# Attention with mixed heads and a gated MLP on one core: the second mixing runs two steps behind the first

## The chip, the cores and the metric

The kernel runs on one core of a Trainium2 chip. The metric is the device time of one execution in microseconds; where several runs are shown, their median. The profile names the engines PE (TensorE, with PEld for its weight loads), DVE (VectorE), ACT (ScalarE), POOL (GpSimd) and SP (SyncE, which issues most DMAs here).

## The reference

Attention over four batches, twelve heads, 448 positions and head size 64, in which the heads are mixed twice: the scores by `w_pre` ahead of the softmax, the weights by `w_post` behind it. Its output is the input of a normalised, gated MLP.

```
scores = scale * matmul(q, k.T)                       # per head
scores = einsum('bhij,hg->bgij', scores, w_pre)       # first mixing
attn   = exp(scores - max) / (sum + 1e-9)             # softmax over j
attn   = einsum('bhij,hg->bgij', attn, w_post)        # second mixing
x      = matmul(attn, v)      -> (1792 tokens, 768)
xn     = x / sqrt(mean(x*x) + 1e-6) * rms_g
out    = (silu(xn @ w_gate) * (xn @ w_val)) @ w_out   # 768 -> 1536 -> 768
```

## The kernel before

**Chunks and steps.** The query rows of a batch are cut into four chunks (120, 120, 120 and 88 rows), sixteen chunks in all (`n` = 0 to 15). A chunk is worked off in steps `p` (six, and five in the last chunk of a batch), 92 steps in all. `steps` numbers them, and `first[n]` is the number of the first step of chunk `n`: `first[14]` is 81 and `first[15]` is 87. `part_a` runs a loop over `t`, and one turn of it is called step t here.

**A turn of the loop.** The order in which the turns issue their instructions is each engine's order; nothing moves them afterwards. In turn t stand, on their engines:

- `premix` (line 187): TensorE's first mixing of step t, into two banks `sp`. Woven into it are the score matmuls `qk_mm` (line 140) of a later chunk, whose two banks `qk` go out through `qk_evac`: one half as `st` on ACT (line 162), the other on DVE (line 160). SP then lays the `st` tiles into the rows `r` of a later step by DMA (line 179).
- `rowmax` (DVE, line 196: two negated row maxima `nm`), `expo` (ACT, line 203: two tiles `e` of exponentials, and their sums), and `norm`: on DVE `t` and `rp` (lines 210, 212), on POOL two tiles `wn` (line 215), which are `w_post` scaled by the reciprocal of the sums.
- `postmix` (line 226): the second mixing, of step t-1, 56 matmuls with `e` as the loaded weights and `wn` as the moving operand, into two banks `pm`. `evac_a` copies one of them to `at_all` on ACT (line 265), the other on DVE (line 263).
- `av_mm` (line 294): the product with v, in units that `av_at` lays out over the turns. A block is two chunks (the last two chunks are blocks of their own) and has twelve units, two for each pair of heads. After four units the two banks `av` are full, and ACT copies them to `xt` (lines 304, 306, 308); the copy stands at the head of the turn after the units.
- POOL adds and squares `xt` (lines 318 to 333) for the sums that the normalisation needs, and SP stores `xt` (lines 340, 343). `sq_all` turns the column sums of a batch (`pss`, line 347, on TensorE) into reciprocal roots, in small operations over several turns.

PSUM has two banks for each of `qk`, `sp`, `pm` and `av`, so that each of these waits for the copies or exponentials of what it held before. In SBUF four tiles `e` are kept.

**After the loop's end** comes part B, the MLP (lines 741 to 752 on TensorE). Its first weights and factors are prepared by DVE, ACT and POOL in the last turns of the loop.

## Time and profile before

| what | value |
| --- | --- |
| median of 3 runs | 827.72 us (825.3 to 830.05) |
| the profiled execution | 822.48 us |
| its span in the trace | 820.6 us |
| PE busy | 794.4 us, 97% of the span |
| DVE busy | 634.5 us, 77% |
| ACT busy | 507.3 us, 62% |
| POOL busy | 350.4 us, 43% |
| mean granted clock of TensorE | 0.998 |

The span is from the first to the last instruction in the trace; that execution took 1.9 us more than its span. The loop over the steps runs from 20.1 us to about 339 us of the span, and the MLP from there to the end. A busy share is an average over both.

### The profile page before, as it was taken

The page shows a single profiled execution, that of the slowest core. Times are in us where ns is not written, and L with a number is a line of the kernel's source. Part 1 is how long each engine was busy: PE and PEld are TensorE (multiplying, and loading weights), DVE is VectorE, ACT ScalarE, POOL GpSimd, SP SyncE. Part 2 cuts the span into 40 slices and gives each one's busy share as a digit, 9 for nine tenths or more (in the row PEclk, how much of TensorE's full clock was granted, in tenths as well). Part 3 has the DMA queues.
Part 4 walks back from the last instruction along what each step waited for, and adds up shares of the span by engine and source line. Part 5 has one row for each costly group of instructions (what it writes and reads, how often), then busy time and mean ns, then how long its engine had stood idle before and what let it go on. Part 6 is the DMA issues. An engine that isn't in the chain of part 4 may idle for free.

```text
span 820.6 us, 26914 instructions
## 1 busy us (share of the span) xinstructions
PE 794.4 (97%) x10806; PEld 485.2 (59%) x10806; DVE 634.5 (77%) x1322; ACT 507.3 (62%) x1133; POOL 350.4 (43%) x467
## 2 busy tenths in 40 slices
PE   7899999999999989899999999999999999999998
PEld 2567777767776767655555555555555555555555
DVE  5777878888798867888788978997889676547562
ACT  3677778777776867664344454545444546969850
POOL 7212343454355435843624433426144359452310
PEclk9999999999999999999999999999999999999999
DMA  7777777777876754564255644754546446566641
GB/s 216 208 216 217 219 229 222 228 219 232 222 234 200 211 147 150 158 230 118 66 177 150 183 129 127 216 149 121 174 145 201 133 127 184 157 199 176 184 135 67
DMA packets 81902, 145.15 MB, mean 177 GB/s; under 512 B 10527, under 2 KB 72797, under 8 KB 81779
## 3 DMA queue, kind: packets, MB, share of 16 engines
q1 hardware_dynamic: 79982, 139.83, 57.0%
q0 software_dynamic: 832, 2.06, 1.0%
q8 instruction: 85, 1.39, 0.7%
q10 hardware_dynamic: 965, 1.56, 0.6%
q14 instruction: 38, 0.31, 0.1%
HBM read 72.83 MB, written 31.88 MB: 128 GB/s over the span
## 4 chain that ended last, share of the span: by engine, by line
PE 86%; DMA 8%; DVE 2%; issue 1%; ACT 1%; POOL 1%; SPq 0%; ACTq 0%; DVEq 0%; POOLq 0%
PE qk L140 7%; PE pm L226 7%; PE sp L187 7%; PE av L294 6%; PE pg L750 6%; PE pg L752 6%; PE pv L752 6%; PE pg L751 6%; PE pv L751 6%; PE pv L750 6%; DMA r<-st 6%; PE po L751 6%; PE po L750 6%; PE po L752 6%; DMA wraw<-in_wgv 1%
## 5 line engine op out<-in xcount | busy, mean ns | idle before, releaser
L187 PE MATMUL sp<-r,wk_pre 64*64 64x448 f32 x720 | 167.4, 542 | 5.4 <-DMA r<-st 3.5
L203 ACT ACTIVATE e<-sp,nm 128x448 f32<-128x448 f32 x180 | 114.3, 637 | 84.8 <-DVE nm L196 82.4
L140 PE MATMUL qk<-k,q 64*64 64x448 f32 x768 | 152.6, 559 | 5.9 <-DMA q<-in_q 4.1
L196 DVE TENSOR_REDUCE nm<-sp 128x1 f32<-128x448 f32 x180 | 110.3, 620 | 44.1 <-PE sp L187 27.4
L215 POOL TENSOR_SCALAR wn<-wk,rp 128x60 f32<-128x60 f32 x180 | 59.5, 345 | 181.8 <-DVE rp L212 109.7
L226 PEld LDWEIGHTS pm<-wn,e 60*64 60x64 f32 x5040 | 106.1, 134 | 37.6 <-POOL wn L215 23.8
L226 PE MATMUL pm<-wn,e 60*64 60x60 f32 x5040 | 106.7, 220 | 4.2 <-issue 4.1
L798 POOL TENSOR_TENSOR sg<-sg,u 128x448 f32<-128x448 f32 x36 | 45.9, 1275 | 151.2 <-ACT sg L795 106.7
L294 PE MATMUL av<-at_all,v 64*64 64x240 f32 (+6 forms) x1728 | 93.6, 316 | 4.6 <-issue 2.6
L750 PE MATMUL pv<-x,wh 128*128 128x448 f16 x264 | 93.0, 352 | 0.0
L752 PE MATMUL pv<-x,wl 128*128 128x448 f16 x264 | 93.0, 352 | 0.0
L752 PE MATMUL pg<-x,wl 128*128 128x448 f16 x264 | 93.0, 352 | 0.0
L751 PE MATMUL pv<-x,wh 128*128 128x448 f16 x264 | 93.0, 352 | 0.0
L751 PE MATMUL pg<-x,wh 128*128 128x448 f16 x264 | 93.0, 352 | 0.0
L750 PE MATMUL pg<-x,wh 128*128 128x448 f16 x264 | 93.0, 352 | 0.0
L750 PE MATMUL po<-h,fac 128*128 128x448 f16 (+1 forms) x258 | 89.8, 348 | 0.0
L751 PE MATMUL po<-h,fac 128*128 128x448 f16 (+1 forms) x258 | 89.8, 348 | 0.0
L752 PE MATMUL po<-h,fac 128*128 128x448 f16 (+1 forms) x258 | 89.8, 348 | 0.0
L750 PEld LDWEIGHTS <-wh 128*128 128x128 f16 x528 | 51.7, 98 | 48.2 <-issue 0.2
L751 PEld LDWEIGHTS <-wh 128*128 128x128 f16 x528 | 51.7, 98 | 48.3 <-issue 0.3
L752 PEld LDWEIGHTS <-wl 128*128 128x128 f16 x528 | 51.7, 98 | 48.2
L187 PEld LDWEIGHTS sp<-r,wk_pre 64*64 64x64 f32 x720 | 60.3, 133 | 27.2 <-ACT e L203 13.2
(167 smaller groups left out, 1567.3 us busy)
## 6 DMA issues: line engine op xcount, KB each, us to landing
r<-st SPq DMA_DIRECT2D x117, 210.0 KB
hraw<-td SPq DMA_DIRECT2D x84, 224.0 KB
wraw<-in_wgv SPq DMA_DIRECT2D x20, 768.0 KB
td<-keep SPq DMA_DIRECT2D x48, 224.0 KB
wraw<-in_wo SPq DMA_DIRECT2D x12, 768.0 KB
r<-st SPq DMA_DIRECT2D x44, 157.5 KB
v<-in_v SPq DMA_DIRECT2D x24, 256.0 KB
k<-in_k SPq DMA_DIRECT2D x24, 224.0 KB
```

Source lines behind the costliest of these rows:

```text
L140: nc.tensor.matmul(ps[j][m, :S], qt[n][sl, hp, m], kt[n // NC, hp][sl], start=True, stop=True)
L187: nc.tensor.matmul(o, wk_pre[sl], rt[n][sl, 2 * p + v_], start=True, stop=True)
L196: nc.vector.tensor_reduce(t, ps[:, :S], AX.X, ALU.max, negate=True)
L203: nc.scalar.activation(e, ps[:, :S], AF.Exp, bias=nmx.pop((n, p, u)), accum_out=sm[n, p][:, u : u + 1])
L215: nc.gpsimd.tensor_scalar(wn[n, p][:, u], wk, r[:, u : u + 1], 1.0, ALU.mult, ALU.mult)
L226: nc.tensor.matmul(o[:, :, at_], e_[sl, j : j + JT], w_[sl].rearrange("p (s i) -> p s i", s=2), start=True, stop=True)
L294: nc.tensor.matmul(x, vt[b, hp][sl, j, c_], a, start=(c_ == 0), stop=(c_ == JC - 1))
L750: nc.tensor.matmul(ps, a, xh[:, kk, at_], start=(kk == 0), stop=False)
L751: nc.tensor.matmul(ps, a, xl_[:, kk, at_], start=False, stop=False)
L752: nc.tensor.matmul(ps, a2, xh[:, kk, at_], start=False, stop=(kk == KT - 1))
L798: nc.gpsimd.tensor_tensor(h, sg, u, ALU.mult)
```

## The change

From turn 2 to turn 84 `postmix` and `evac_a` are those of step t-2, where they were those of step t-1. Turn 85 (`near`, the fifth turn of chunk 14, the last chunk but one) does both step 83 and step 84, with the copies of step 83 between the two; from turn 86 on they are those of step t-1 again, as before. So that the product with v stays behind the second mixing, the early blocks' units of `av_mm` begin and end one turn later, block 5 begins one turn later, and block 6 (chunks 12 and 13) begins at turn 83 in place of 82 and ends where it did; the chains of `sq_all` of the first two batches stand one turn later too. There are six tiles `e` in place of four, and the DMA scratch is set to 8192, which frees SBUF.

```diff
-            e = pe.tile([128, S], F32, name="e", tag="e", bufs=4)
+            e = pe.tile([128, S], F32, name="e", tag="e", bufs=6)
...
+    mix_at = [[] for _ in range(T + 40)]
+    near = first[14] + 4
+    for i, step in enumerate(steps):
+        mix_at[i + 2 if i < near - 2 else max(i + 1, near)].append(step)
     for blk, ns in enumerate(BLOCKS):
-        lo = first[ns[-1] + 1] + 1
-        hi = first[ns[-1] + (3 if ns[-1] < 13 else 2)] + 1
+        lo = first[ns[-1] + 1] + (1 if first[ns[-1] + 1] >= near else 2)
+        hi = first[ns[-1] + (3 if ns[-1] < 13 else 2)] + (2 if ns[-1] < 11 else 1)
...
     for b in range(B - 1):
-        t = first[NC * b + NC + 2] + (5 if b < B - 2 else 3)
+        t = first[NC * b + NC + 2] + (6 if b < B - 2 else 3)
...
-            if back(1):
-                postmix(*back(1))
+            for a in mix_at[t]:
+                postmix(*a)
+                if a is not mix_at[t][-1]:
+                    for v_ in range(2):
+                        evac_a(*a, v_)
             for a in av_at[t]:
                 av_mm(*a)
...
-            if back(1):
+            for a in mix_at[t][-1:]:
                 for v_ in range(2):
-                    evac_a(*back(1), v_)
+                    evac_a(*a, v_)
...
-    nc = bacc.Bacc("TRN2", target_bir_lowering=False, num_devices=1)
+    nc = bacc.Bacc("TRN2", target_bir_lowering=False, num_devices=1, dynamic_dma_scratch_size=8192)
```

TensorE at the loop's start, as a difference: turn 1 (the first mixing `sp` of step 1 with the scores `qk` of chunk 2), and then turn 2.

```order
 L187 MATMUL sp<-r_121,wk_pre 64x448 x2
 L140 MATMUL qk<-k_0_130,q_242 64x448 x2
-L226 MATMUL pm<-wn,e 64x2x30 x28
 L187 MATMUL sp<-r_121,wk_pre 64x448 x2
 L140 MATMUL qk<-k_1_132,q_242 64x448 x2
```

Turn 1 has no second mixing any more, and each one after it stands one turn later.

TensorE in turns 84 and 85, before. `pss` are the column sums of a batch and end turn 84; the numbers behind `v_` tell the pairs of heads of block 6 apart.

```order
L226 MATMUL pm<-wn,e 64x2x30 x28
L294 MATMUL av<-at_all,v_2_6272 64x240 x12
L294 MATMUL av<-at_all,v_2_6272 64x2x60 x4
L347 MATMUL pss<-ones,sum_5224 112x1 x4
L187 MATMUL sp<-r_123,wk_pre 64x448 x4
L226 MATMUL pm<-wn,e 64x2x30 x28
L294 MATMUL av<-at_all,v_3_6429 64x240 x12
L294 MATMUL av<-at_all,v_3_6429 64x2x60 x4
L187 MATMUL sp<-r_123,wk_pre 64x448 x4
```

The same two turns now:

```order
L226 MATMUL pm<-wn,e 64x2x30 x28
L294 MATMUL av<-at_all,v_1_6075 64x240 x4
L294 MATMUL av<-at_all,v_1_6075 64x2x60 x4
L294 MATMUL av<-at_all,v_2_6239 64x240 x8
L347 MATMUL pss<-ones,sum_5260 112x1 x4
L187 MATMUL sp<-r_123,wk_pre 64x448 x4
L226 MATMUL pm<-wn,e 64x2x30 x56
L294 MATMUL av<-at_all,v_2_6239 64x240 x4
L294 MATMUL av<-at_all,v_2_6239 64x2x60 x4
L294 MATMUL av<-at_all,v_3_6396 64x240 x12
L294 MATMUL av<-at_all,v_3_6396 64x2x60 x4
L187 MATMUL sp<-r_123,wk_pre 64x448 x4
```

In turn 84 the last unit on the banks of the first two pairs (`v_1`) is now followed at once by the first unit on the next banks (`v_2`); before, a unit on the banks began only in the turn after the last one on them. Turn 85 has two second mixings in one row (x56) and three units where it had two.

ACT in turns 84 and 85, before; `xt` are the copies of the `av` banks.

```order
L304 ACTIVATE xt_6944<-av 128x480
L304 ACTIVATE xt_6945<-av 128x480
L203 ACTIVATE e,s<-sp,nm 128x448 x2
L162 ACTIVATE st<-qk 128x448
L265 ACTIVATE at_all<-pm 128x2x42x5
L203 ACTIVATE e,s<-sp,nm 128x448 x2
L265 ACTIVATE at_all<-pm 128x2x42x5
L304 ACTIVATE xt_7127<-av 128x480
L304 ACTIVATE xt_7128<-av 128x480
```

And now:

```order
L203 ACTIVATE e,s<-sp,nm 128x448 x2
L162 ACTIVATE st<-qk 128x448
L265 ACTIVATE at_all<-pm 128x2x42x5
L304 ACTIVATE xt_7002<-av 128x480
L304 ACTIVATE xt_7003<-av 128x480
L203 ACTIVATE e,s<-sp,nm 128x448 x2
L265 ACTIVATE at_all<-pm 128x2x42x5 x2
L304 ACTIVATE xt_7124<-av 128x480
L304 ACTIVATE xt_7125<-av 128x480
```

The two copies that free the first `av` banks of block 6 stood ahead of the exponentials of turn 84 and now stand behind the `at_all` copy of that turn; in turn 85 two `at_all` copies stand behind the exponentials.

## Rows read from the trace of the kernel before

**Rows 1.** Waits of all engines: total us, times, longest.

```profile
engine line waited for: us in total, times, longest us
PEld pm L226 <- POOL wn L215: 23.8, 65, 1.1
```

**Rows 2.** Timeline of one turn: start us, us, engine, line, operation, [idle before <-releaser].

```profile
119.96 0.59 PE L140 MATMUL qk<-k,q 64*64 64x448 f32 x2
...
120.43 0.55 ACT L265 ACTIVATE at_all<-pm 128x420 f32<-128x420 f32 x1
...
120.83 0.60 POOL L215 TENSOR_SCALAR wn<-wk,rp 128x60 f32<-128x60 f32 x2 [3.18 <-PE sp L187]
...
121.02 0.54 PE L140 MATMUL qk<-k,q 64*64 64x448 f32 x2
...
121.39 1.01 PE L226 MATMUL pm<-wn,e 60*64 60x60 f32 x51
...
121.72 0.62 DVE L196 TENSOR_REDUCE nm<-sp 128x1 f32<-128x448 f32 x1 [0.27 <-PE sp L187]
...
122.26 0.61 DVE L160 COPY st<-qk 128x448 f32<-128x448 f32 x1
...
123.05 0.54 PE L140 MATMUL qk<-k,q 64*64 64x448 f32 x1
```

**Rows 3.** Timeline of PE, two early turns without a product with v.

```profile
48.32 0.54 PE L187 MATMUL sp<-r,wk_pre 64*64 64x448 f32 x1
...
51.38 0.54 PE L187 MATMUL sp<-r,wk_pre 64*64 64x448 f32 x1
```

**Rows 4.** Timeline of two turns: `wn` early (140.18) and late (256.65).

```profile
140.18 0.60 POOL L215 TENSOR_SCALAR wn<-wk,rp 128x60 f32<-128x60 f32 x2 [2.16 <-DVE rp L212]
...
140.66 0.65 PE L140 MATMUL qk<-k,q 64*64 64x448 f32 x2
...
141.04 0.33 PE L226 MATMUL pm<-wn,e 60*64 60x60 f32 x4
...
256.43 0.54 PE L140 MATMUL qk<-k,q 64*64 64x448 f32 x2
...
256.65 0.60 POOL L215 TENSOR_SCALAR wn<-wk,rp 128x60 f32<-128x60 f32 x2 [2.38 <-DVE stats L669]
...
257.02 0.26 PE L226 MATMUL pm<-wn,e 60*64 60x60 f32 x1
```

**Rows 5.** The chain that ended last, third turn: start us, us, what.

```profile
26.01 4.74 DMA r<-st
```

**Rows 6.** Timeline of PE, end of turn 84 to start of turn 87.

```profile
309.96 0.95 PE L347 MATMUL pss<-ones,sum 128*112 128x1 f32 x8
310.84 0.98 PE L187 MATMUL sp<-r,wk_pre 64*64 64x448 f32 x8
311.64 0.99 PE L226 MATMUL pm<-wn,e 60*64 60x60 f32 x54
...
312.46 1.64 PE L294 MATMUL av<-at_all,v 64*64 64x240 f32 x31
314.43 1.58 PE L187 MATMUL sp<-r,wk_pre 64*64 64x448 f32 x8 [0.32 <-ACT e L203]
315.94 1.08 PE L226 MATMUL pm<-wn,e 60*64 60x60 f32 x55
...
318.23 0.60 PE L187 MATMUL sp<-r,wk_pre 64*64 64x448 f32 x4
```

**Rows 7.** Timeline of ACT and DVE, turns 84 and 85.

```profile
306.35 1.03 ACT L304 ACTIVATE xt<-av 128x480 f32<-128x480 f32 x2
...
309.60 0.60 ACT L265 ACTIVATE at_all<-pm 128x420 f32<-128x420 f32 x1
...
312.96 1.13 DVE L196 TENSOR_REDUCE nm<-sp 128x1 f32<-128x448 f32 x2
...
314.89 0.53 ACT L265 ACTIVATE at_all<-pm 128x420 f32<-128x420 f32 x1
```

**Rows 8.** Windows: length, busy us (x) of PE, PEld, DVE, ACT, POOL, granted clock, DMA share, GB/s.

```profile
330.00:334.00 4.00, 2.43 (x89) 2.23 (x90) 3.90 (x6) 2.09 (x6) 3.46 (x4) 0.85 0.20 66
334.00:338.00 4.00, 4.00 (x107) 3.03 (x100) 1.72 (x6) 1.83 (x7) 2.08 (x4) 0.73 0.51 149
345.00:820.60 475.60, 472.40 (x2624) 247.24 (x2622) 360.70 (x618) 263.20 (x484) 194.32 (x145) 1.00 0.51 156
```

**Rows 9.** Waits of SP's queue: total us, times, longest.

```profile
SPq L340 <- POOL xt L318: 24.2, 7, 6.8
```

**Rows 10.** DMA issues of POOL's queue: KB each, median us to landing.

```profile
r<-st POOLq DMA_DIRECT2D x4, 210.0 KB, 7.3
```

## The prediction

> **What bounds the kernel now.** I read the windows first, to part the span into its stages. From 345 us to the end TensorE is busy 472.40 of 475.60 us at full clock [rows 8]: part B is bound by TensorE, so what happens in the loop reaches the end only as a shift of part B's start. The change touches the loop alone, so I went on to its waits.

> The list of waits names the one that the change aims at: the weight loads of the second mixing wait 65 times, 23.8 us in all, for POOL's `wn` [rows 1]. That would be some 3% of the run if TensorE stood still meanwhile. Whether it does, the timeline of a turn tells [rows 2]. The last pair of matmuls of the woven stream starts at 121.02, the second mixing at 121.39, 0.37 later; `wn` came from 120.83 on, two halves in 0.60, so its first half at about 121.13. The wait of the load ended there, while the stream was still running. So I need a turn in which `wn` came early: there it was ready from 140.48 on, and the second mixing started at 141.04, again 0.38 behind the last pair at 140.66 [rows 4]. Early or not, it starts when the stream lets it. In the same group is a turn in which `wn` does hold it: 257.02 against 256.43, 0.59, so 0.21 lost.

> What sets the turn instead is seen in early turns that have no product with v: the first mixing starts at 48.32 and at 51.38, 3.06 apart [rows 3]. The loop behind this runs over DVE: scores, first mixing, second row maximum at 121.72 (0.62), the copy `st` at 122.26 (0.61, to 122.87), and the next scores at 123.05, of which the last can't start before that bank is copied [rows 2]. From 119.96 to 123.05 it is 3.09, in a turn that has products with v, so these hardly lengthen it. None of it passes through `wn` or the second mixing.

> The last turns are another stage. In turn 86 TensorE waits for `e` and then for `wn` [rows 6], and at 330 to 334 it is busy 2.43 of 4.00 us, while DVE has 3.90 [rows 8].

> **The change part by part.** *Steady turns.* The second mixing has its `wn` a turn ahead. Taken away is 0.21 in the turns that look like the one at 257.02; walking through the timelines I found a handful of these, so five times 0.21, 1.0 us. Bounds: nothing, if the next wait ends as late (the `at_all` copy that frees the second mixing's bank ends at 120.98 [rows 2], 0.15 ahead of `wn`'s first half), and 65 times 0.21, 13.7, if every wait listed were worth as much. I take 1.0, since 0.37 and 0.38 say that most are worth nothing.

> [...]

> *The loop's start.* Turn 1 has no second mixing. The chain's next large piece is a DMA of 4.74 us from 26.01 on, for which turn 3 waits [rows 5]; TensorE's time saved in turn 1 ends in that wait. Nothing; at most the 0.8 us of one second mixing.

> *Turn 84.* Now the unit that fills the first `av` banks of block 6 and the first unit on the next use of them stand in one turn. The latter waits for the copies `xt`, which ACT has behind its `at_all` copy. That ends at 310.20 (309.60 and 0.60), and the two copies take 1.03 [rows 7]: 311.23. Before, they were done at 307.38 and nobody waited. A unit takes 0.73: from the second mixing's start at 315.94 to the next first mixing at 318.23 is 2.29, of which the second mixing takes 0.82 (311.64 to 312.46), and two units the rest [rows 6]. So the column sums start at 311.96 in place of 309.96, 2.0 later. At that point one unit less has been done, at most 0.73 back; but turn 82, left without units, is then set by the 3.06 of [rows 3], and turn 83 has three, so I take 0.2 back. **+1.8** (1.3 to 2.0).

> *Turn 85.* The second mixing of step 84 needs the banks of step 83's, which both copies must empty. ACT's stands behind two exponentials that wait for the row maxima, and ended at 314.89 plus 0.53, 315.42 [rows 7]; DVE's stands behind two row maxima, which ended at 314.09, and is done sooner. From 315.42 come the second mixing, 0.82, and three units, 2.20: the first mixing of turn 86 starts at 318.44, in place of 314.43 [rows 6]. **+4.0**. (Turn 84's delay adds to both sides.) The units can't fill the gap: they stand behind the second mixing in TensorE's order. Bounds: the gap between 312.46 and 315.42 alone, 3.0, and 4.0 with the extra unit, which is the one that turn 84 was short of.

> *Turn 86.* There the second mixing started 1.51 behind the first (315.94 less 314.43), against 0.80 in turn 85 [rows 6]: it waited 0.7 for `wn` of the step before. Now TensorE arrives later and finds it ready: **-0.7** (0 to -0.7).

> *Nothing* I put for the rest. Two more `e` tiles remove no wait that sets a turn, and only make room for the lag. The stores of `xt` and POOL's sums shift by a turn; SP waits 24.2 us for these sums already, in 7 places, the longest 6.8 [rows 9], and one such wait moved in front of a load of `r` could cost its 6.8 once. [...]

> *The sum.* -1.0 + 1.8 + 4.0 - 0.7 = **+4.1 us**. Is it handed on? The turns behind have DVE at 3.90 of 4.00 and part B has no slack [rows 8], so yes. The profiled execution took 822.48 us and would take 826.6. It is 0.6% under the median of the runs shown; on the median, 827.72 and 4.1 make **831.8 us**.

> **The rivals.** I call half a per cent, 4.1 us, what a measurement of this kernel can just tell from no change.

> *Faster: the wait is real.* Where the load's wait holds TensorE in more turns than I saw, the steady term grows to as much as 13.7, and with the tail's 5.1 the run loses 8.6 us: 813.9 on the profiled execution, 819.1 on the median. It decides from 5.1 over 65 turns on, 0.08 a turn. For it: 23.8 us in 65 waits [rows 1]; several steady turns end near `wn`. Against: 0.37 and 0.38, and the 3.06 of turns which `wn` doesn't reach. Half of its size, 825, would still be the same side.

> *Slower than I say.* Turn 84 costs its 2.0, turn 86 gives nothing back, the steady turns gain nothing, and the gaps bring the clock down. [...] 2.0 + 4.0 + 1.1 = 7.1: 829.6 there, 834.8 on the median. For it: two gaps of 2 to 3 us close together. [...]

> *No change: the tail swallows it.* DVE, ACT and POOL prepare part B in the same turns. If they use TensorE's gaps to work ahead, the 1.6 us for which TensorE stands at 330 to 334 [rows 8] and more behind it shrink by as much as the gaps cost. Then -1 to +1: 822.5, or 827.7. Against: each engine's order is fixed, and much of that work stands behind operations of the late turns.

> **How the numbers follow.** My forecast, +2.5 to +5.5, has 0.38, a little over half of it below 4.1. Faster has 0.2, and a tenth of it would stay within half a per cent; slower 0.2; no change 0.22. So faster by over half a per cent 0.18, within it 0.45, slower 0.37. The predicted time is that of the forecast, 831.8. The range goes from 822, which leaves out the larger half of the faster rival, to 838, which adds half of one long wait of SP's queue to the slower one's 834.8. The forecast's own range is 830 to 833.5.

> **What would show it.** In the profile after, the waits of the second mixing's loads for `wn` nearly vanish, and the turns keep 3.06 us: then the main step is right. TensorE should show a gap ahead of a unit of `av` at about 310 that ends with ACT's `xt`, and one of some 3 us about 4 us on, within the double second mixing, that ends with an `at_all` copy. The MLP should start some 4 us later. I am wrong if the turns are shorter than before between 60 and 290 us, or if the two gaps are there and the MLP starts no later.

## The result and the profile after

The changed kernel takes 833.5 us (median of 20 runs), the kernel before 827.17 us (20 runs): ratio 1.0082, 95% interval 1.006 to 1.0105. That is 6.8 us slower, inside the forecast range, with the forecast sign and above its size of 4.1. One of the 20 runs before took 4612.52 us and stands outside of the ratio. The profiled execution of after took 833.15 us with a span of 831.3. The one of before was among its quickest (822.48), so the difference of these two traces, 10.7 us, is more than the change costs, and stretches of before are read below from a second kernel with the same instructions too (f1_side).

The waits of all engines, after (engine, line, releaser: us in all, times, longest). They answer to [rows 1]:

```profile
PEld pm L226 <- issue: 21.9, 58, 2.6
PEld pm L226 <- POOL wn L215: 6.7, 20, 0.8
```

The wait for `wn` has gone from 23.8 us in 65 places to 6.7 in 20, as the change means it to. In its place stands "issue", 21.9 us in 58 places (8.2 in 22 before): the load waits for nothing that the profile shows. The early turns, on TensorE's timeline of after, answer to [rows 3]:

```profile
48.96 0.54 PE L187 MATMUL sp<-r,wk_pre 64*64 64x448 f32 x1
...
52.03 0.54 PE L187 MATMUL sp<-r,wk_pre 64*64 64x448 f32 x1
```

They are 3.07 us apart, where they were 3.06. The end of turn 84 to the start of turn 87, the same view; it answers to [rows 6]:

```profile
315.04 1.49 PE L294 MATMUL av<-at_all,v 64*64 64x240 f32 x16 [1.41 <-ACT xt L304]
316.45 1.24 PE L347 MATMUL pss<-ones,sum 128*112 128x1 f32 x8
317.63 1.77 PE L187 MATMUL sp<-r,wk_pre 64*64 64x448 f32 x8
319.17 1.76 PE L226 MATMUL pm<-wn,e 60*64 60x60 f32 x56
322.18 1.81 PE L226 MATMUL pm<-wn,e 60*64 60x60 f32 x56 [1.25 <-ACT at_all L265]
323.69 3.97 PE L294 MATMUL av<-at_all,v 64*64 64x240 f32 x48
327.45 0.96 PE L187 MATMUL sp<-r,wk_pre 64*64 64x448 f32 x8
...
330.44 1.09 PE L187 MATMUL sp<-r,wk_pre 64*64 64x448 f32 x8
```

Both forecast gaps are there, 1.41 us that ends with ACT's `xt` and 1.25 us (some 3 by the forecast) that ends with an `at_all` copy. And what stands between them takes nearly twice its time, from the first mixing on: eight matmuls of the first mixing 1.77 in place of 0.98, a second mixing 1.76 in place of 0.99 [rows 6]. The windows of after show why (length, then busy us of PE, PEld, DVE, ACT, POOL, granted clock, DMA share, GB/s):

```profile
310.00:314.00 4.00, 3.63 (x98) 2.45 (x90) 2.36 (x5) 1.77 (x5) 1.11 (x2) 1.00 0.45 139
314.00:318.00 4.00, 2.96 (x28) 2.15 (x32) 0.40 (x3) 1.44 (x4) 0.60 (x2) 0.87 0.26 77
318.00:322.00 4.00, 2.94 (x64) 1.83 (x56) 3.07 (x10) 1.79 (x5) 0.00 (x0) 0.50 0.02 8
322.00:326.00 4.00, 3.82 (x84) 3.56 (x88) 1.48 (x7) 0.57 (x2) 0.81 (x4) 0.50 0.02 4
326.00:330.00 4.00, 4.00 (x109) 3.38 (x106) 1.55 (x3) 1.87 (x5) 2.48 (x4) 0.85 0.36 94
```

Behind the first gap the granted clock falls from 1.00 to 0.50, and stays there over the second gap: by the windows for some 10 us (8 at 0.50, and 0.13 and 0.15 of 4 us under 1.00 on either side, which would be 1.0 and 1.2 us at 0.50).

To set these stretches beside the experiments, I read from TensorE's timeline of every kernel the starts of the first mixing of turns 5, 81, 84 and 86, and the end of the last second mixing:

| kernel | turns 5 to 80, us | turns 84 and 85, us | turn 81 to the last second mixing, us | ratio to before |
| --- | --- | --- | --- | --- |
| before | 257.45 | 8.48 | 45.76 | 1 |
| f1_side | 262.98 | 8.41 | 44.63 | 1.0003 |
| f2_avshift | 262.86 | 8.41 | 44.98 | 1.0012 |
| f4_phase_lag1 | 261.87 | 8.51 | 44.63 | 1.0159 |
| after | 261.10 | 17.31 | 52.13 | 1.0082 |
| e1_units | 266.67 | 11.87 | 48.96 | 1.0068 |
| e2_between | 262.70 | 12.58 | 50.94 | 1.0089 |
| e3_both | 269.44 | 10.44 | 47.41 | 1.0115 |
| e4_near14 | 259.66 | 8.48 | 48.39 | 1.0083 |
| f3_phase_lag2 | 259.67 | 8.48 | 45.05 | 1.0122 |
| e8_fill | 267.87 | 14.70 | 48.94 | 1.0084 |
| h1_wide_lag1 | 253.91 | 8.41 | 44.49 | 0.9849 |
| h2_wide_lag2 | 252.24 | 16.97 | 50.89 | 0.9919 |
| h3_wide_both | 248.83 | 10.34 | 47.32 | 0.9879 |

The second and third columns repeat where the instructions of these turns do; the first does not: after, e1_units, e2_between and e3_both have the same instructions there, and differ by 8 us.

### The profile page after: what moved, and what is told of

It is laid out like the page before. It is cut to its first block, busy times and chain, and to the rows that moved or that the text cites. A ratio compares the mean times of both kernels' runs of the same rounds, so it can differ in the third digit from the quotient of the medians.

```text
span 831.3 us, 26909 instructions
## 1 busy us (share of the span) xinstructions
PE 801.7 (96%) x10806; PEld 492.0 (59%) x10806; DVE 632.2 (76%) x1322; ACT 507.1 (61%) x1133; POOL 351.1 (42%) x467
## 3 DMA queue, kind: packets, MB, share of 16 engines
q8 instruction: 85, 1.39, 0.7%
## 4 chain that ended last, share of the span: by engine, by line
PE 87%; DMA 5%; DVE 3%; issue 2%; ACT 1%; POOL 1%; ACTq 1%; SPq 0%; DVEq 0%; POOLq 0%
PE qk L140 8%; PE pm L226 8%; PE sp L187 7%; PE av L294 7%; PE pg L757 6%; PE pv L757 6%; PE pv L759 6%; PE pg L759 6%; PE pg L758 6%; PE pv L758 6%; PE po L759 6%; PE po L758 6%; PE po L757 6%; DMA r<-st 2%; DMA xr<-xd 1%
## 5 line engine op out<-in xcount | busy, mean ns | idle before, releaser
L226 PEld LDWEIGHTS pm<-wn,e 60*64 60x64 f32 x5040 | 112.0, 136 | 38.1 <-issue 21.9
L226 PE MATMUL pm<-wn,e 60*64 60x60 f32 x5040 | 108.4, 222 | 9.1 <-issue 7.7
L294 PE MATMUL av<-at_all,v 64*64 64x240 f32 (+6 forms) x1728 | 95.3, 319 | 4.7 <-issue 3.1
L294 PEld LDWEIGHTS av<-at_all,v 64*64 64x64 f32 x1728 | 71.1, 135 | 9.5 <-issue 6.2
```

The costliest lines, as they stand in the source:

```text
L226: nc.tensor.matmul(o[:, :, at_], e_[sl, j : j + JT], w_[sl].rearrange("p (s i) -> p s i", s=2), start=True, stop=True)
L294: nc.tensor.matmul(x, vt[b, hp][sl, j, c_], a, start=(c_ == 0), stop=(c_ == JC - 1))
```

## The experiments

### Taking the tail's waits away

The theory "tail" puts the whole loss on the waits of turns 84 and 85 and the clock behind them; the rival "lag" puts it on the steady turns. **e1_units** lays block 6's units out as 4, 2, 2, 2, 2:

```diff
-            t = lo + i * (hi - lo) // len(units)
+            t = lo + (i * (hi - lo) // len(units) if blk != 6 else max(i // 2 - 1, 0))
```

> The change with block 6's units of the product with v laid out as 4, 2, 2, 2, 2 over turns 83 to 87 in place of 3, 2, 3, 2, 2, so that no unit waits for the xt copies in turn 84 and turn 85 has two units. The double second mixing in turn 85 stays. Theory 'tail' (the whole loss is the two waits in turns 84 and 85 with the clock that falls behind them, the steady turns give about 1 us): the gap of 1.4 us before the unit in turn 84 is gone, the granted clock falls less or not at all, and the run stands about 3 us (2 to 4.5) over the kernel before. Rival 'lag' (the two-step lag costs time in the steady turns too, since the trace of after was already 4.2 us late at turn 84): 5 to 8 us over the kernel before.

Measured: 1.0068 (1.0034 to 1.0102), 5.6 us. The two turns took 11.87 us in place of 17.31, with one gap ahead of the second of the two mixings and the granted clock at 1.00:

```profile
325.54 1.03 PE L226 MATMUL pm<-wn,e 60*64 60x60 f32 x54 [2.95 <-ACT at_all L265]
```

In time that is the rival's 5 to 8 us, with an interval (2.8 to 8.4 us) that reaches into the theory's 2 to 4.5. In its trace the steady turns took 266.67, more than in after.

**e2_between** puts turn 85's units between its second mixings:

```diff
             for a in mix_at[t]:
+                if a is mix_at[t][-1] and len(mix_at[t]) > 1:
+                    for a_ in av_at[t]:
+                        av_mm(*a_)
                 postmix(*a)
...
-            for a in av_at[t]:
+            for a in av_at[t] if len(mix_at[t]) < 2 else []:
                 av_mm(*a)
```

> The change with turn 85's units of the product with v put between its two second mixings, so that they cover the wait for the at_all copies. The wait for the xt copies in turn 84 stays. Theory 'tail': the gap of 1.25 us between the two second mixings is gone, the gap in turn 84 and some of the fall of the clock stay, about 4 us (2.5 to 5.5) over the kernel before. Rival 'lag': 6 to 8 us over it.

Measured: 1.0089 (1.0052 to 1.0127); the two turns took 12.58 us. On TensorE's timeline the first gap is as in after, the second is down to 0.68, and the work between them takes its usual 0.95 to 0.98:

```profile
316.15 1.49 PE L294 MATMUL av<-at_all,v 64*64 64x240 f32 x16 [1.41 <-ACT xt L304]
317.57 0.95 PE L347 MATMUL pss<-ones,sum 128*112 128x1 f32 x8
318.45 0.98 PE L187 MATMUL sp<-r,wk_pre 64*64 64x448 f32 x8
...
323.00 1.03 PE L226 MATMUL pm<-wn,e 60*64 60x60 f32 x54 [0.68 <-ACT at_all L265]
```

So the clock stayed up here behind the same first gap (windows of e2):

```profile
313.00:317.00 4.00, 2.59 (x82) 1.92 (x76) 1.90 (x5) 3.15 (x8) 0.60 (x2) 1.00 0.19 60
317.00:321.00 4.00, 4.00 (x108) 3.12 (x104) 2.24 (x10) 0.00 (x0) 0.00 (x0) 1.00 0.22 68
```

**e3_both** has both edits.

> Both of these at once: neither wait is left, and everything else is the change, steady turns and loop start among it. Theory 'tail': no gap in turns 84 and 85, granted clock 1.0 there, and a run within 2 us of the kernel before (-2 to +2). Rival 'lag': still 4 us or more over it.

Measured: 1.0115 (1.0074 to 1.0156). The two turns took 10.44 us, 6.9 less than in after, and the time did not fall. On TensorE's timeline the first gap is gone, but units weren't enough to cover the second:

```profile
324.25 1.65 PE L294 MATMUL av<-at_all,v 64*64 64x240 f32 x31
327.42 1.03 PE L226 MATMUL pm<-wn,e 60*64 60x60 f32 x54 [1.52 <-ACT at_all L265]
```

**e4_near14** moves the double turn to 81:

```diff
-    near = first[14] + 4
+    near = first[14]
```

> The change with the turn that does two second mixings moved from 85 to 81, the first turn of chunk 14; block 6 then begins at turn 82 as before, and turns 82 to 91 are the kernel before's. There is one unit of the product with v in turn 81. Theory 'tail': the wait between the two second mixings comes once, without units to lengthen it and without the column sums ahead of it, 0 to 3 us over the kernel before. Rival 'lag': 4 us or more over it.

Measured: 1.0083 (1.0054 to 1.0112). Turns 84 and 85 are back at 8.48 us; the double second mixing waits 1.24 us in turn 81 for an `at_all` copy, and the clock stays up. Its profiled execution was its quickest run of 12 (826.66, median 832.66). By these four "tail" alone had failed: their stretch from turn 81 on is 1.2 to 4.7 us shorter than in after, and their times are not. e3 and e4 lie clear of what it expected; e1 and e2 lie above it, with intervals that reach into it. The four were not timed beside the change itself but each beside before, so the difference of two ratios is uncertain by some 3 to 4 us, about as much as was taken away.

### What lengthens the steady turns

In all these traces TensorE stands now and then, mostly with "issue" as the reason: by the lists of waits its matmuls stand so for up to 1.1 us in before, 1.8 in after and 3.5 in e3_both. A piece of after's timeline:

```profile
138.69 0.40 PE L226 MATMUL pm<-wn,e 60*64 60x60 f32 x10
140.52 0.86 PE L226 MATMUL pm<-wn,e 60*64 60x60 f32 x44 [1.43 <-issue]
```

I numbered TensorE's instructions in the order in which they start (matmuls, weight loads, and 298 waits for semaphores and the like that its queue has between them), and listed the gaps over 0.06 us in which neither a matmul nor a load runs. Gaps of one sort stand at the same place in every 256 instructions: in before 12 of them in turns 5 to 80, and 16 in after. In turns 5 to 80, counting those at that place that end 1.2 to 1.8 us behind the end of an instruction packet, of which more below:

| kernel | gaps at that place | their sum, us | turns 5 to 80 without them, us |
| --- | --- | --- | --- |
| before | 12 | 8.4 | 249.1 |
| f1_side | 17 | 12.6 | 250.4 |
| f2_avshift | 17 | 9.3 | 253.5 |
| f4_phase_lag1 | 17 | 13.7 | 248.2 |
| after | 16 | 11.1 | 250.0 |
| e1_units | 16 | 15.7 | 251.0 |
| e2_between | 14 | 10.1 | 252.6 |
| e3_both | 18 | 15.1 | 254.4 |
| e4_near14 | 15 | 9.8 | 249.9 |
| f3_phase_lag2 | 14 | 11.9 | 247.8 |
| e8_fill | 19 | 14.0 | 253.9 |
| h1_wide_lag1 | 0 | 0.0 | 253.9 |
| h2_wide_lag2 | 1 | 0.4 | 251.9 |
| h3_wide_both | 0 | 0.0 | 248.8 |

The page's list of DMA queues (packets, MB, share of 16 engines) has two queues for instructions. The larger is the same in before and after:

```profile
q8 instruction: 85, 1.39, 0.7%
```

85 packets in 1.39 MB are 16 KB each, and TensorE has 10806 matmuls, as many loads and 298 of those waits, which is 85.6 times 256. So by my estimate a packet is 256 of its instructions, which is also how far apart the gaps stand. In the trace of before one packet starts between any two of these boundaries, 1.9 us on average after the first of them was passed (0.3 to 4.3), and takes 1.2; where TensorE stood, it went on 1.3 to 1.7 us after the packet's end. The boundaries are 5.0 us apart. Where TensorE stood, the packet had started 2.5 us after the boundary, elsewhere 1.7; with its 1.2 and the 1.3 to 1.7 behind its end, 2.5 comes to 5.0 to 5.4, and 1.7 to 4.2 to 4.6. From these numbers I estimate that a packet that starts late is not there in time. That is the suspect: a stall that comes to 11.1 us in after and to 15.7 in e1_units, with the same instructions in these turns, and that a change of order may move.

Four runs asked what of the change moves it. **f1_side** is the kernel before with the side edits alone:

```diff
-            e = pe.tile([128, S], F32, name="e", tag="e", bufs=4)
+            e = pe.tile([128, S], F32, name="e", tag="e", bufs=6)
...
-    nc = bacc.Bacc("TRN2", target_bir_lowering=False, num_devices=1)
+    nc = bacc.Bacc("TRN2", target_bir_lowering=False, num_devices=1, dynamic_dma_scratch_size=8192)
```

> The kernel before (lag of one turn everywhere) with six tiles e and the DMA scratch of 8192, nothing else. Four versions of the change, with and without its tail, all stood 0.7 to 1.2% over the kernel before, and their traces show more time lost at TensorE's code boundaries (every 256 of its instructions). Theory 'side edits': this alone costs 0.5% or more. Rivals 'lag', 'products' and 'code phase': no difference, within 0.3%.

Measured: 1.0003 (0.997 to 1.0037). No cost, within some 3 us.

**f2_avshift** is the change with the old lag:

```diff
-        mix_at[i + 2 if i < near - 2 else max(i + 1, near)].append(step)
+        mix_at[i + 1].append(step)
...
-        lo = first[ns[-1] + 1] + (1 if first[ns[-1] + 1] >= near else 2)
+        lo = first[ns[-1] + 1] + (1 if blk > 5 else 2)
```

> The change with the lag of the second mixing put back to one turn; the products with v of blocks 0 to 5, their copies, stores and sums stay one turn later as in the change, the side edits stay too. Theory 'products' (the stores and loads that move a turn delay TensorE's code loads): 0.5 to 1% over the kernel before. Theory 'lag' (the second mixing's lag itself): no difference, within 0.3%. Theory 'code phase' (which instruction falls on a boundary): either.

Measured: 1.0012 (0.9983 to 1.0041). No cost that stands clear of the noise either (3.4 us at most, by the interval): the loss does not come with the later products, stores and sums, and what remains is the lag and its tail.

**f3_phase_lag2** and **f4_phase_lag1** shift the boundaries, by 28 and by 36 more matmuls ahead of turn 0 (the first in the version e4, as shown; the second in the kernel before, with 40 matmuls of 44 columns):

```diff
-        for _ in range(4):
-            nc.tensor.matmul(busy[:, :S], ones, kt[0, 0], start=True, stop=True)
+        for _ in range(32):
+            nc.tensor.matmul(busy[:, :56], ones, kt[0, 0][:, :56], start=True, stop=True)
```

> The version with the double turn at 81 (lag of two turns up to there, tail of the kernel before), and the four filler matmuls ahead of turn 0 cut into 32 small ones of as many columns in sum: 112 more TensorE instructions, so that the code boundaries fall in each turn where they fell before the change took the second mixing out of turn 1. Theory 'code phase': back to the kernel before, within 0.3%. Theory 'lag': still 0.6 to 1% over it.

> The kernel before with the four filler matmuls cut into 40 small ones of as many columns in sum: 144 more TensorE instructions, which with 256 to a boundary puts the boundaries of the early turns where the change has them. Theory 'code phase': 0.5 to 1% over the kernel before. Theory 'lag': no difference, within 0.3%.

Measured: 1.0122 (1.0066 to 1.0179) and 1.0159 (1.0113 to 1.0204), and the runs miss their question. The small fillers took 13.29 us at a granted clock of 0.50, where the four large ones took 3.27 at 1.00 (before, from 16.90), as f3's timeline and windows show:

```profile
17.03 13.29 PE L494 MATMUL busy<-k,ones 128*128 128x56 f32 x64
```

```profile
18.00:22.00 4.00, 4.00 (x20) 4.00 (x20) 0.00 (x0) 0.00 (x0) 3.21 (x6) 0.50 0.71 220
22.00:26.00 4.00, 4.00 (x20) 4.00 (x21) 0.00 (x0) 0.00 (x0) 0.00 (x0) 0.50 0.94 225
```

Turn 5 starts 10.1 and 12.5 us late, about the whole of 10.1 and 13.2 us by the ratios. What is left, 0.0 and 0.6 us with 4 to 5 to either side, is too uncertain to tell the theories apart.

### The same turns with fewer instructions

**h1_wide_lag1**, **h2_wide_lag2** and **h3_wide_both** take the boundaries out of the question: as many columns, in fewer matmuls. They leave the second and third block of each tile of exponentials out of the product, so what they return is not the reference's result.

```diff
             for u in range(2):
-                for c in range(JC):
+                for c in (0, JC - 1):
...
+            x = w_[sl].rearrange("p (s i) -> p s i", s=2)
+            if c == 0 and len(e) > 1:
+                x = x.unsqueeze(2).to_broadcast([HR, 2, JC - 1, HR // 2])
+                nc.tensor.matmul(o[:, :, at_ : at_ + JC - 1], e_[sl, j : j + JT], x, start=True, stop=True)
```

> The kernel before with the second mixing of every full step in 12 matmul calls in place of 28, as many columns streamed: a call over the first block of exponentials writes the columns of three blocks, so the second and third block of each tile of exponentials are left out of the product. TensorE's work in columns stays, its instructions per turn fall from about 176 to 112. Theory 'code loads' (some 14 us of the steady turns are stalls at code boundaries): the stalls nearly vanish and the run is 8 to 18 us under the kernel before. Rival 'columns' (the turns are set by TensorE's columns and by DVE): within 3 us of it.

> The change with the same second mixing (the same part left out). With the code stalls gone, what the change does stands clear of them: theory 'tail' expects it 5 to 9 us over the wide version with the lag of one turn, all of it in turns 84 and 85, and the steady turns within 2 us of each other; rival 'lag' expects the steady turns longer by 3 us or more; rival 'the wait for wn was real' expects them shorter by 3 us or more.

> The version without both tail waits (units 4, 2, 2, 2, 2 and the units of turn 85 between its two second mixings), with the same second mixing (the same part left out). Theory 'tail': 3 us or less over the wide version with the lag of one turn, so 4 to 6 us under the wide version of the change. Rival 'lag': as slow as the wide version of the change, within 2 us.

Measured: 0.9849 (0.9812 to 0.9887), 0.9919 (0.9887 to 0.995) and 0.9879 (0.9844 to 0.9914). The page of h1 has 63 code packets in place of 85, for 7990 matmuls, as many loads and the 298 waits, which are 63.6 times 256:

```profile
q8 instruction: 63, 1.03, 0.5%
```

The gaps at that place of the 256 are gone (none in h1 and h3, one of 0.4 us in h2), and the run is 12.5 us shorter, though TensorE streams as many columns and `wn` is still waited for, as h1's list of waits says:

```profile
PEld pm L229 <- POOL wn L215: 27.2, 69, 1.1
```

The wide second mixing, with 24 matmuls and as many loads in place of 56, is itself a little shorter too: it takes 0.73 us from its start to the next first mixing (50.40 to 51.13 in h1), where it took 0.82 (50.56 to 51.38 in before). Over 88 full steps that could be up to 8 of the 12.5 us. The traces speak for the stalls: without the gaps at the boundaries turns 5 to 80 take 248.8 to 253.9 us in the wide kernels and 247.8 to 254.4 in the others. No run parts the two causes.

With the stalls gone the three stand in the order of the theory "tail". The change is 0.70% over the old lag, 5.8 us; the version without the tail's waits 0.30%, 2.5 us. The three were timed beside each other, so their means can be compared directly: h2 is 6.0 us over h1 and 3.6 over h3, each with 2.9 or less to either side, which is clear, the second just so; h3 over h1, 2.4 with 2.9 to either side, is not. Their traces agree: from turn 81 on 6.4 us and 2.8 us more than h1. The steady turns are 1.7 and 5.1 us shorter than h1's, so the lag itself costs nothing here. A gain isn't shown either, since h2 and h3 have the same instructions in these turns and differ by 3.4.

### The clock

**e8_fill** is the change with two filler matmuls in each gap:

```diff
                     for v_ in range(2):
                         evac_a(*a, v_)
+                    fill(2)
             for a in av_at[t]:
+                if t == near - 1 and a is av_at[t][-1]:
+                    fill(2)
                 av_mm(*a)
```

> The change with two filler matmuls in front of the unit that waits in turn 84 and two between the two second mixings of turn 85, 1.6 us of work each, so that TensorE is busy in most of both waits. Theory 'tail, with the clock': the granted clock stays near 1.0 through turns 84 and 85 and the two turns together shrink from 17.3 us to about 13.5. Rival 'waits alone': the clock had no part, the two turns stay at 17 us or get longer by what the fillers add.

Measured: 1.0084 (1.0046 to 1.0123), no gain in time, with 267.87 us in its steady turns. But in the two turns, which it is about, the clock stays up (windows of e8):

```profile
314.00:318.00 4.00, 3.58 (x102) 2.75 (x94) 2.36 (x5) 1.91 (x7) 1.54 (x4) 1.00 0.43 137
318.00:322.00 4.00, 3.88 (x32) 2.26 (x36) 0.36 (x3) 1.40 (x4) 0.60 (x2) 1.00 0.26 80
322.00:326.00 4.00, 3.21 (x68) 1.74 (x60) 3.01 (x10) 1.76 (x5) 0.00 (x0) 1.00 0.01 4
```

The two turns take 14.70 us, 2.6 less than in after, with the fillers in them. So the fall of the clock is at least 2.6 us of the 8.8 by which they grew in the trace of after. That the fillers prevented it can't be told from one trace: e2 keeps its clock there without any, and so do e1, e3 and e4 (1.00 in the windows of each over its gaps), while h2 loses it like after (0.50 from 306 to 314). The timed runs say more: the mean granted clock of a run is 1.000 in six of e8's eight, in none of after's 20 (0.992 to 0.998), and in 3 of 16 of the kernel before in e8's session. With the clock up the change is still 0.84% over before, so the clock seems to be a small part of the loss in the timed runs.

## Why the prediction was right, and where it was not

**Steady turns, -1.0.** The reading held: the waits for `wn` were nearly all covered, the period of the early turns did not change, and no trace shows the 13.7 us of the faster rival. (Half of that wait, 6.9 us, would have made 826.0, not 825.) The size is below what these runs can show. What I didn't see is a part of the steady turns' length: not DVE's loop alone, but the gaps at every 256 of TensorE's instructions, 8.4 to 15.7 us of turns 5 to 80 in the kernels with the narrow second mixing. In h1, with 63 packets in place of 85, these stalls are gone. That a late packet makes them is my estimate.

**The loop's start, 0.** Turn 5 starts at 36.82, at 36.18 before and 36.26 in f1_side; no gain.

**Turn 84, +1.8.** It grew by 2.6 us, from 4.89 to 7.49 (310.14 to 317.63 in after). The wait is the forecast one, and ends when the first of the two copies is done. But the unit behind it takes 1.41 us to the column sums (315.04 to 316.45), where I had put 0.73, and does so at full clock too: 1.42 in e2, whose turn 84 takes 7.19. So 0.5 us over the forecast come from this unit, and 0.3 from the clock, which falls during the column sums (1.18 us to the next first mixing in after, 0.88 in e2). One half of the unit's matmuls writes the bank that the second copy empties, 0.4 us later, at 315.45; that this is the reason is not shown.

**Turn 85, +4.0.** It grew by 6.2 us, from 3.59 to 9.82. This is the term that was mis-sized for the profiled execution. I had put the clock into the slower rival alone, at 1.1 us. No run shows that term: in after the clock's fall came to at least 2.6 us, and in e1 to e4 the clock stayed at 1.00 behind the gaps. In e8, where the clock stays up, turn 85 takes 7.43 us, 3.8 more than before, which is the forecast 4.0 (its fillers end ahead of the copy):

```profile
321.66 0.98 PE L187 MATMUL sp<-r,wk_pre 64*64 64x448 f32 x8
326.22 1.03 PE L226 MATMUL pm<-wn,e 60*64 60x60 f32 x54 [1.01 <-ACT at_all L265]
329.09 1.01 PE L187 MATMUL sp<-r,wk_pre 64*64 64x448 f32 x8
```

Up to the second of the two mixings the slow clock costs nothing: 4.55 us in after, 4.56 in e8, since both gaps end with ACT's `at_all` copy (1.25 and 1.01 us); the slower first mixings only shorten the gap, from the 2.95 that e1 shows at full clock to 1.25. From there to turn 86 it is 5.27 us against 2.87.

**Turn 86, -0.7.** It took 2.99 in place of 3.79: -0.8.

**Handed on.** Nearly: of the 8.8 us, turn 86 and the later ones gave back 0.8 and 0.8 to 1.6, since TensorE waits in the last turns anyway: in before, from 318 to 345, its loads stand 3.1 us for POOL's `wn` and 2.3 for DVE's `wl`, and its matmuls 0.4 for ACT's `x`. The last second mixing ends at 350.05 us, at 339.39 before and 343.88 in f1_side, and part B starts behind it. From turn 81 on after is 6.4 to 7.5 us longer than before and f1_side. That this equals the measured 6.8 us is in part luck, since most timed runs had less of the clock's fall than this trace.

**The sum.** +4.1 forecast, 6.8 measured (5.0 to 8.7 by the interval). At full clock the tail's terms come to 3.7 to 4.5 us: 2.3 of turn 84 (e2), 3.8 of turn 85 (e8), -0.8 of turn 86 and -0.8 to -1.6 behind it. That is the forecast's mechanism at about its size. The clock adds 2.6 us or more in the profiled execution. Its mean granted clock is 0.994, for which its fall of some 10 us accounts (half of 10.2 in 831.3 us is 0.6%). 14 of the 20 timed runs have 0.996 or 0.998, too high for a fall so long, and they are hardly quicker: 833.2 us on average, and 833.9 the other six. Over all timed runs the mean is 0.9957, against 0.9965 in 64 runs of the kernel before, a difference worth some 0.6 us. So some 2 us of the 6.8 have no source that is shown, though the interval is as wide. The side edits cost nothing, as said (f1_side, f2_avshift).

**What stays open.** e1 to e4 removed 1.2 to 4.7 us of the tail and ran no faster. In e3_both the ratio leaves some 7 us that its tail (2.8 us over f1_side) doesn't explain, and its trace has 6.5 us more in turns 5 to 80 than f1_side: 2.5 of it at the code boundaries, and 3.3 in one wait of turn 81's first mixing for the DMA of `r`. (In the trace of after the longest wait for `r` in these turns is 1.0.) Seven traces with the longer lag have 263.9 us there on average (259.7 to 269.4), four with the old lag 261.3 (257.5 to 263.0): a difference of 2.6 us in a spread of 4, 1.5 of it at the boundaries (12.5 against 11.0) and 1.1 in the rest (251.4 against 250.3). It may be that a TensorE that doesn't wait for `wn` meets the boundaries more often, since in the wide versions, without stalls, the lag costs nothing; that is argued, not shown. The runs that were to shift the boundaries were spoilt by their fillers. For the kernel as it is, then, the two waits at the seam are shown in the trace, but no version with less of them ran clearly faster than the change.

## What to carry to other kernels

A wait in the list is worth what TensorE would do without it: set the start of the waiting instruction against the end of the stream ahead of it, in a turn with the wait and in one without. A change of pipeline depth can pay at its seam (here turns 84 and 85 took 17.31 us in place of 8.48), so cost the turn in which the depth changes instruction by instruction, with the engine's order of copies, and allow in the range for the clock, which may or may not fall behind a gap (behind one of 1.41 us it fell to 0.50 in after, and stayed at 1.00 in e2). And where a loop of many small matmuls stalls with "issue" at regular distances, fewer and wider instructions can be worth more than a reordering of waits: here 1.5% for a quarter fewer (63 packets in place of 85), in a version that leaves part of the product out.
